# Hourglass attention and a phase MLP: four heads per load, two row blocks per store, and a new written order

## The chip, the cores and the metric

The kernel runs on one core of a Trainium2 chip. The core has five engines with queues of their own: TensorE (PE, matrix products, with its weight loads as PEld), VectorE (DVE), ScalarE (ACT), GpSimd (POOL) and SyncE (SP, which here only issues DMAs). The metric is the device time of one execution in microseconds (us).

## What is computed

```python
def sm_attn(qq, kk, vv):                      # softmax attention, scale 1/8
    ...
q_d = q.reshape(B, H, Sd, factor, D).mean(axis=3)      # factor 4; k_d, v_d alike
out_d = sm_attn(q_d, k_d, v_d)
out_up = np.repeat(out_d, factor, axis=2)
mask = np.abs(pos[:, None] - pos[None, :]) < factor    # local attention: 3 keys to either side
...
x = (out_up + out_local)                               # to (B, S, H * D)
theta = x @ w_theta
zr, zi = x * np.cos(theta), x * np.sin(theta)
u = x + np.einsum('ts,bsd->btd', w_tok_r, zr) + np.einsum('ts,bsd->btd', w_tok_i, zi)
return u + np.maximum(u @ w_ch, 0.0)
```

q, k and v are 8 batches x 8 heads x 576 positions x 64, in float32; the token weights are 576 x 576, the other weights 512 x 512; the result is 8 x 576 x 512 float32. The kernel computes in bfloat16 between loads and stores.

## The kernel before, in words

The program is written out in full, without loops at run time. Each kind of work is a generator that yields after each step, and a string, ORDER (L719), names the steps one letter at a time: the n-th occurrence of a letter runs the n-th step of its sequence (L749 to L756). Each step emits its instructions, and `pin` (L734) holds every engine to that order. So one string sets the order of PE, DVE, ACT, POOL and SP at once, and an instruction that waits holds up all that is behind it on its engine. A second string, BANKS (L63), names the PSUM bank (or the first of two) of each accumulator. The text below writes a step as its letter with the batch.

The steps, batch by batch:

- L (`load`, L182) issues the loads on SP: for k and q one DMA for two heads, 128 partitions x 576 float32, 288 KB, into a slot of the pool `stg` (16 slots, L60); for v five windows of 2 x 64 positions, each as two DMAs of 128 KB in rows of 64 values (`values`, L194). C (`cast`, L212) turns each loaded slot into bfloat16: in batch 0 on ACT (k), DVE (q) and POOL (v), afterwards all on POOL (L220, L224).
- A (`turns`, L290) transposes k and q on PE (L305), and ACT evacuates them (L306). a (`sums`) sums four neighbours for the pooled attention, on DVE (L334, L338) or POOL (L343, L344).
- S and P (L425, L401) are the local and the pooled scores with their exponentials on ACT; M (L433) multiplies the local ones by the band mask on DVE. U is the pooled v, V, y, N, x, n are the outputs, their quotients and a transposition; T (L537, L542) transposes and adds both to x.
- H (`phases`, L565 to L582) is x times w_theta, and cosine and sine of it on ACT. Its first step of a batch handles the last 64 positions (the tail) into the tile `cst`, which has one buffer. h (`tail_z`, L585) multiplies that by x into a tile `zT`, also with one buffer, and SP transposes it by a DMA (L591). Z (L617) makes the other z; in batches 6 and 7 the transposes for it are DMAs, J (L605).
- X (`mix`, L627) is the token mix, eight accumulations of nine matmuls of 256 or 320 columns for a batch (L638), each added to x on DVE (L642). r (`residual`, L645) turns the result back by four DMA transposes on SP (L652; in batch 7 on PE) and copies its tail on POOL (L656).
- R (`channels`, L669) multiplies by w_ch; O (`relu`, L689) takes max(.,0) and adds the residual on DVE (L692) into a slot `osb` of 128 x 512 float32, of which there are five; o (`store`, L708) stores each slot, 256 KB, on SP (L710). t, Q, q, s are the same for the tails of two batches at a time.
- l, c, w load, cast and transpose the weights in the same `stg` slots: w_theta first, then the token weights, and w_ch later.

ACT computes exponentials (S, P) and sines (H) from different function tables; a change from one to the other shows as an ACT_TABLE_LOAD.

A slot of a pool is taken by a new tile once the last reader of the old one is done; the first writer of the new one waits for that. `warm_up`, `more_values` and `storing` (L165, L204, L702) have no effect with the settings in this kernel, apart from one memset on DVE.

## Time and profile before

| | us |
|---|---|
| median of 3 runs | 240.19 (237.18 to 241.02) |
| the profiled execution: its time | 240.87 |
| the profiled execution: span from first to last instruction | 239.2 |
| PE busy | 215.0 |
| DVE busy | 191.6 |
| ACT busy | 152.0 |
| POOL busy | 104.6 |

The page of the profile gives each engine's busy time, the chain of work that ended last (followed back from the last instruction, at each step to what released it), and groups of instructions by line with their number, busy time and mean length. A busy PE is not a PE at its peak, since matmuls are pipelined and a waiting one can count as busy. The granted TensorE clock was 1.0 in the whole execution. In the chain and in the timelines a line begins with its start and its length in us; "SPq" is an issue on SP's queue, "issue" is time in which an engine waited for nothing that the profile shows.

### The profile page before, as it was taken

The page shows a single profiled execution, that of the slowest core. Times are in us where ns is not written, and L with a number is a line of the kernel's source. Part 1 is how long each engine was busy: PE and PEld are TensorE (multiplying, and loading weights), DVE is VectorE, ACT ScalarE, POOL GpSimd, SP SyncE. Part 2 cuts the span into 40 slices and gives each one's busy share as a digit, 9 for nine tenths or more (in the row PEclk, how much of TensorE's full clock was granted, in tenths as well). Part 3 has the DMA queues.
Part 4 walks back from the last instruction along what each step waited for, and adds up shares of the span by engine and source line. Part 5 has one row for each costly group of instructions (what it writes and reads, how often), then busy time and mean ns, then how long its engine had stood idle before and what let it go on. Part 6 is the DMA issues. An engine that isn't in the chain of part 4 may idle for free.

```text
span 239.2 us, 8218 instructions
## 1 busy us (share of the span) xinstructions
PE 215.0 (90%) x3370; PEld 154.3 (64%) x3370; DVE 191.6 (80%) x389; ACT 152.0 (64%) x212; POOL 104.6 (44%) x172
## 2 busy tenths in 40 slices
PE   0465998999899989989999999999999989999993
PEld 0443867777578765866577766866677557847751
DVE  5496889989778989866899898998999788665664
ACT  3678678969897886446884976377956953043030
POOL 6323636896857755377377324392163000000000
PEclk9999999999999999999999999999999999999999
DMA  6999999998999999999999939998876656473757
GB/s 201 266 182 321 357 311 159 260 279 157 292 216 217 228 282 185 183 235 299 202 192 277 302 63 210 233 230 223 134 179 109 86 118 180 83 222 67 206 177 256
DMA packets 84229, 50.11 MB, mean 210 GB/s; under 512 B 69216, under 2 KB 69216, under 8 KB 84192
## 3 DMA queue, kind: packets, MB, share of 16 engines
q1 hardware_dynamic: 84192, 49.60, 92.4%
q8 instruction: 26, 0.43, 0.8%
q14 instruction: 11, 0.09, 0.2%
HBM read 34.11 MB, written 9.44 MB: 182 GB/s over the span
## 4 chain that ended last, share of the span: by engine, by line
PE 68%; ACT 9%; DVE 7%; SPq 6%; DMA 3%; issue 3%; POOL 2%; DVEq 0%; ACTq 0%; POOLq 0%
PE psum L638 26%; PE psum L674 11%; PE psum L576 10%; PE psum L305 4%; PE psum L537 3%; SPq L198 3%; DMA st_v<-in_v_dram 2%; PE psum L497 2%; PE psum L616 2%; PE psum L445 2%; DVE tmp L514 2%; PE psum L452 2%; SPq L185 2%; ACT pm L425 1%; PE psum L418 1%
## 5 line engine op out<-in xcount | busy, mean ns | idle before, releaser
L638 PE MATMUL psum<-WT,z 128*128 128x256 bf16 (+1 forms) x576 | 77.0, 286 | 0.1
L638 PEld LDWEIGHTS <-z 128*128 128x128 bf16 x576 | 54.1, 98 | 14.8 <-issue 0.6
L642 DVE TENSOR_TENSOR uT<-psum,xT 128x256 bf16<-128x256 f32 (+1 forms) x64 | 28.9, 454 | 12.6 <-PE psum L638 11.8
L581 ACT ACTIVATE cs<-psum,pihc 128x512 bf16<-128x512 f32 x32 | 22.1, 691 | 21.4 <-PE psum L576 17.2
L224 POOL CAST v_w<-st_v 128x512 bf16<-128x512 f32 x40 | 24.8, 638 | 20.7 <-DMA st_v<-in_v_dram 19.1
L576 PE MATMUL psum<-wth,xT 128*128 128x512 bf16 x128 | 33.1, 387 | 0.1
L674 PE MATMUL psum<-wch,uT 128*128 128x512 bf16 x128 | 31.4, 379 | 0.7 <-ACT cs L582 0.7
L343 POOL TENSOR_TENSOR two<-qT 128x576 f32<-128x576 bf16 x14 | 16.1, 1147 | 27.6 <-ACT qT L306 27.4
L514 DVE TENSOR_TENSOR tmp<-psum,rl 128x512 bf16<-128x512 f32 x40 | 27.3, 684 | 0.7
L220 POOL CAST q_tm<-st_q 128x576 bf16<-128x576 f32 x28 | 21.6, 771 | 12.2 <-DMA st_q<-in_q_dram 11.9
L542 DVE TENSOR_TENSOR xT<-psum,xdT 128x464 bf16<-128x464 f32 (+1 forms) x40 | 24.5, 628 | 2.9 <-PE psum L537 2.5
L425 ACT ACTIVATE pm<-psum 128x1024 bf16<-128x1024 f32 (+1 forms) x24 | 20.5, 881 | 7.6 <-PE psum L418 6.8
L692 DVE SCALAR_TENSOR_TENSOR osb<-psum,ur 128x512 f32<-128x512 f32 x32 | 21.6, 684 | 2.3 <-PE psum L674 1.5
L306 ACT COPY qT<-psum 128x1152 bf16<-128x1152 bf16 x16 | 18.0, 1128 | 7.9 <-PE psum L305 7.9
L656 POOL COPY ut<-uT 128x256 bf16<-128x256 bf16 x8 | 3.4, 428 | 44.9 <-DVE uT L642 44.9
L334 DVE TENSOR_REDUCE kd<-kT 128x290 bf16<-128x1160 bf16 x16 | 21.6, 1353 | 1.6 <-ACT kT L306 1.6
L220 POOL CAST k_tm<-st_k 128x576 bf16<-128x576 f32 x28 | 19.5, 695 | 6.0 <-DMA st_k<-in_k_dram 5.3
L306 ACT COPY kT<-psum 128x1152 bf16<-128x1152 bf16 x16 | 17.9, 1122 | 5.6 <-PE psum L305 3.8
L305 PE MATMUL psum<-ident,k_tm 128*128 128x128 bf16 x144 | 11.9, 234 | 9.4 <-ACT k_tm L220 9.2
L674 PEld LDWEIGHTS <-uT 128*128 128x128 bf16 x128 | 11.8, 98 | 12.3 <-issue 0.8
L617 DVE TENSOR_TENSOR z<-psum,cs 128x1024 bf16<-128x1024 bf16 x24 | 16.3, 685 | 4.0 <-ACT cs L582 2.0
L582 ACT ACTIVATE cs<-psum 128x512 bf16<-128x512 f32 x32 | 19.1, 597 | 0.0
(87 smaller groups left out, 358.7 us busy)
## 6 DMA issues: line engine op xcount, KB each, us to landing
...
st_k<-in_k_dram SPq DMA_DIRECT2D x32, 288.0 KB, 4.9
st_q<-in_q_dram SPq DMA_DIRECT2D x32, 288.0 KB, 5.1
...
stw_tok<-in_moe_w_tok_r_dram SPq DMA_DIRECT2D x4, 288.0 KB, 6.6
stw_tok<-in_moe_w_tok_i_dram SPq DMA_DIRECT2D x4, 288.0 KB, 6.0
...
```

Of the source, the lines that this page charges most:

```text
L220: eng[i](out=dst[:, hh // 2, :, hh % 2, :], in_=staged.pop((b, f"{nm}{hh}")).rearrange("p (r d) -> p r d", d=D))
L224: eng[2](out=v_w[:, c, :, 0:D], in_=staged.pop((b, f"v{c}"))[:, 0:DM].rearrange("p (h d) -> p h d", d=D))
L306: EVAC[n](out=To[:, 2 * i:2 * i + 2, 0:S].rearrange("p a (w r) -> p a w r", r=WR), in_=ps[:, 0:P * WR].rearrange("p (r a w) -> p a w r", a ...
L334: nc.vector.tensor_reduce(out=kd_groups(kd)[:, 2 * i * NCH:2 * i * NCH + 2 * NCH, 0:PG], axis=AX.X, op=ALU.add, in_=kT[:, hs, :].rearrange ...
L425: nc.scalar.activation(out=pm.rearrange("p e c j w -> p e (c j w)"), in_=ps[:, :, 0:4 * W * n], func=AF.Exp, scale=SCL)
L514: nc.vector.tensor_tensor(out=tmp.rearrange("p g (j d) -> p g j d", d=D), in0=pv[:, :, :, 0:D], in1=rl.unsqueeze(3).to_broadcast([P, 2, 4, ...
L542: nc.vector.tensor_tensor(out=xT[:, :, CH * c:CH * c + cnt].rearrange("p e (m j) -> p e m j", j=4), in0=ps[:, :, 0:cnt].rearrange("p e (m ...
L576: nc.tensor.matmul(out=th, lhsT=xT[:, dc, P * c:P * c + P], rhs=wth[:, dc, :], start=(dc == 0), stop=(dc == 3),)
L581: nc.scalar.activation(out=cs[:, 0, :], in_=th, func=AF.Sin, bias=pihc, scale=1.0)
L638: nc.tensor.matmul(out=ps[:, 0:cnt], lhsT=z[:, j, P * dc:P * dc + P], rhs=WT[:, j, cols], start=(j == 8), stop=(j == 0),)
L642: nc.vector.tensor_tensor(out=uT[:, dc, cols], in0=ps[:, 0:cnt], in1=xT[:, dc, cols], op=ALU.add)
L674: nc.tensor.matmul(out=psr, lhsT=uT[:, dc, P * c:P * c + P], rhs=wch[:, dc, :], start=(dc == 0), stop=(dc == 3),)
```

## The change

1. From batch 1 on, one DMA loads four heads of k or q (576 KB) in place of two. Batch 0 keeps its loads.
2. The staging pool has 8 slots of two planes in place of 16 slots of one. k and q share a slot by two head pairs, v by windows (4), (3, 2), (1, 0), weights by two.
3. From batch 1 on, one cast on POOL handles a pair: 4 casts for k and q in place of 8, and 3 for v in place of 5.
4. Two blocks of 128 result rows share a slot of `osb`, three slots of 128 x 2 x 512, and one DMA stores both (512 KB); batch 7 still stores each block by itself. A tail block takes a whole slot.
5. `tail_z` writes its product into `cst` in place, so that `zT` has no tile of its own.
6. ORDER and BANKS are new throughout. In ORDER the letters v and D go, L has 76 steps in place of 104, C 62 in place of 104, o 18 in place of 32.
7. The code without effect is removed, with the memset.

```diff
-    stg = ctx.enter_context(tc.tile_pool(name="stg", bufs=16))
+    stg = ctx.enter_context(tc.tile_pool(name="stg", bufs=8))
...
-    def stage(b, key):
-        t = staged[b, key] = stg.tile([P, S], FP32, tag="st", name=f"st{b}_{key}")
-        return t
+    def stage(b, nm, i):
+
+        if (b, nm, i // 2) not in staged:
+            staged[b, nm, i // 2] = stg.tile([P, 2, S], FP32, tag="st", name=f"st{b}_{nm}{i // 2}")
+        return staged[b, nm, i // 2][:, i % 2, :]
 
     def load(b):
         for hh in range(4):
             for nm, src in (("k", k), ("q", q)):
-                nc.sync.dma_start(out=stage(b, f"{nm}{hh}"),
-                                  in_=src[b, 2 * hh:2 * hh + 2].rearrange("h (p r) d -> (h p) (r d)", r=WR))
-                yield
+                t = stage(b, nm, hh)
+                if b == 0:
+                    nc.sync.dma_start(out=t, in_=src[b, 2 * hh:2 * hh + 2].rearrange("h (p r) d -> (h p) (r d)", r=WR))
+                elif hh % 2 == 0:
+                    nc.sync.dma_start(out=staged[b, nm, hh // 2],
+                                      in_=src[b, 2 * hh:2 * hh + 4].rearrange("(x h) (p r) d -> (h p) x (r d)",
+                                                                              x=2, r=WR))
+                if b == 0 or hh % 2 == 0:
+                    yield
...
+                elif hh % 2 == 0:
+                    eng[i](out=dst[:, hh // 2].rearrange("p r e d -> p e r d"),
+                           in_=staged[b, nm, hh // 2].rearrange("p e (r d) -> p e r d", d=D))
+                    yield
...
+                lo, n = cs[-1], len(cs)
+                eng[2](out=v_w[:, lo:lo + n, :, 0:D],
+                       in_=staged[b, "v", lo // 2][:, 0:n, 0:DM].rearrange("p e (h d) -> p e h d", d=D))
+                yield
...
     def tail_z(b):
-        zT = moep.tile([P, 4, 2, HALF], BF16, tag="zT", bufs=1, name=f"zT_{b}")
+        zT = csts.pop(b)
...
     def relu(b):
         for c in range(4):
-            osb = osbs[b, c] = moep.tile([P, DM], FP32, tag="osb", bufs=5, name=f"osb{c}_{b}")
+            if c % 2 == 0:
+                osbs[b, c // 2] = moep.tile([P, 2, DM], FP32, tag="osb", bufs=3, name=f"osb{c}_{b}")
...
     def store(b):
         for c in range(4):
-            storing(b).dma_start(out=out[b, P * c:P * c + P, :], in_=osbs.pop((b, c)))
-            yield
+            osb = osbs[b, c // 2]
+            if b == B - 1:
+                nc.sync.dma_start(out=out[b, P * c:P * c + P, :], in_=osb[:, c % 2, :])
+                yield
+            elif c % 2 == 1:
+                nc.sync.dma_start(out=out[b, P * c - P:P * c + P, :].rearrange("(e p) d -> p e d", e=2), in_=osb)
+                yield
...
     ORDER = (
-        "LLLLCCLCACLLLLLlLaCCCAACaCLALaaSlMPVySLCcMSVyCMCCPUVlycllllNlVxcNLcLxcVccycLlCnTLCCCTyTwTwHTwHcAwZwH"
...
-        "yrLXyXLTrXLSSSLCoVhyoTXXLLLLTrTRHMZMHLHZZRHoOOaRACaaRZLOCAOCAXCAaXXVCCVyCPrLyaLLaUVMrLoSyPXraXNCNxCr"
...
-        "XTrTTXHoJJMCJCHJMCXhQVyqPRSVyMrrorOUXVrVoyVyHHNxNxRZHZnsTrZZyRRTHXToTTXXJJJJXXOXrhoXXOtOHRHooOZZRRHo"
-        "HRrQrrZZXXOXoOrXOXXrqXXrRrrRRrrOootsQROOqRsROoRoOOosROOooooo"
+        "lLLCLLLLLCCACLLAClCCLaLLLaCCLAAScaCSSlalcMCVPPCMClylVMVylUyllcCcLcVylNLxcNxcVAlnTcCTwTyHwHcwTTlZwcwl"
+        "wHcHwACwLLLwZZcHALchawCwwZwwwLwLwwXaLCLLAXLXLaLaCSSMCCXMSPCCLMXCPVVUyVyyNxNxAVAnLTyLLLXLHTTAAHHaaaaS"
+        "hVyXZCZCCSCMXPPTrVCULCTHLyNNxCHAxZZnAlTXXAaXAMaaCLLXXVSylLLalSXcCMPPcVrLyXlLTSSCVMyLrXHcTVyVChrUHCyH"
...
+        "rOORrRXsOXOnLStSTrXSaVPCMTyMCXXVyPVTXrrTToXyHJJVUyMXNJxNxJHhHVyVVRORoyOnTRTrZrHrZHHZZRTyTXXTXJXOJJJX"
+        "XhXXHHRORHZZHZZRORoXXoOQqXrrOXXrrOorXXXQRrrrtRroqrsOtOQRRRRsRRqOoOsOOOoOoooo"
     )
```

Three places of the new order, with letters resolved to steps (letter, batch, step within the batch; loads and casts left out), beside the old one:

```
about batch 2's first scores
before: X0.6 X0.7 y1.4 S2.0 r0.0 P2.0 S2.1 M2.0 P2.1 Z1.0 V2.0 U2.0 T1.4 H1.3
after:  S2.0 h1.0 V1.4 y1.4 X0.6 Z1.0 Z1.1 S2.1 M2.0 X0.7 P2.0 P2.1 T1.3 r0.0 V2.0 U2.0 T1.4 H1.3
about batch 7's scores and batch 6's phases (S, P and H alone)
before: S7.0 S7.1 P7.0 H6.0 H6.1 P7.1 S7.2 H6.2 H6.3 H6.4
after:  S7.0 S7.1 S7.2 P7.0 P7.1 H6.0 H6.1 H6.2 H6.3 H6.4
the first loads (SP)
before: k0 q0 k1 q1 k2 q2 k3 q3 v4 v3 theta0 v2 v1 v0 theta1
after:  theta0 k0 q0 k1 q1 k2 q2 k3 q3 v4 theta1 v3 v2 v1 v0
```

More of the change, by code (lines that the diff above doesn't have):

```diff
@@ L63 @@
     BANKS = (
-        "0240202460245020462345012346705234501423501634501234560134062046204623024062450145602146050240627645"
-        "0426304323426324062046320462320134621024601245012034615036123204632302460234501203420532043603623046"
-        "2306423402460324602546504236243024350246501240634304350365320462106724067062346534052635206134201240"
-        "63204632014051024124670246102410234502362703202010140123452323010102301302401201"
+        "0240204620462304206452345263470123540612305103456731240563124026124601240264012301460124607416204106"
+        "7206423702630243204630462304623046120312467016207612302024604134024016204620145672356037452304304260"
+        "4526045206420620463245301340256702546540724650450264026540214260526401520642034672304273016403121460"
+        "24062320463201304123042304620123042501425142121212301241525205023230145012301456"
     )
@@ L159 @@
     PU = [PU[0], PU[1], PU[1], PU[1], PU[2]]
-    warm = const.tile([P, 256], BF16, name="warm")
-    nc.vector.memset(warm, 0.0)
-    def warm_up():
-        for i, n in enumerate(WARM):
-            ps = w1(f"wu{i}")
-            for _ in range(n):
-                nc.tensor.matmul(out=ps[:, 0:256], lhsT=ident, rhs=warm, start=True, stop=True)
-            yield
-    WARM = []
     staged, inputs = {}, {}
-    def stage(b, key):
-        t = staged[b, key] = stg.tile([P, S], FP32, tag="st", name=f"st{b}_{key}")
-        return t
+    def stage(b, nm, i):
+        if (b, nm, i // 2) not in staged:
+            staged[b, nm, i // 2] = stg.tile([P, 2, S], FP32, tag="st", name=f"st{b}_{nm}{i // 2}")
+        return staged[b, nm, i // 2][:, i % 2, :]
     def load(b):
@@ L184, in load @@
             for nm, src in (("k", k), ("q", q)):
-                nc.sync.dma_start(out=stage(b, f"{nm}{hh}"),
-                                  in_=src[b, 2 * hh:2 * hh + 2].rearrange("h (p r) d -> (h p) (r d)", r=WR))
-                yield
+                t = stage(b, nm, hh)
[7 more added lines that the diff above has]
+                    yield
         for c in BACK:
-            if HALVES[b] > 0:
-                stage(b, f"v{c}")
-                values(nc.sync, b, c, range(HALVES[b]))
-                yield
+            stage(b, "v", c)
+            values(nc.sync, b, c, range(2))
+            yield
     def values(queue, b, c, halves):
-        t = staged[b, f"v{c}"][:, 0:DM].rearrange("p (h d) -> p h d", d=D)
+        t = stage(b, "v", c)[:, 0:DM].rearrange("p (h d) -> p h d", d=D)
         for g in halves:
@@ L198, in values @@
             queue.dma_start(out=t[W * g:W * g + W], in_=v[b, :, lo:lo + W, :].rearrange("h p d -> p h d"))
-    HALVES = [2, 2, 2, 2, 2, 2, 2, 2]
-    def more_values(b):
-        for c in BACK:
-            if HALVES[b] < 2:
-                if HALVES[b] == 0:
-                    stage(b, f"v{c}")
-                values(nc.scalar, b, c, range(HALVES[b], 2))
-                yield
     def cast(b):
@@ L219, in cast @@
             for i, (nm, dst) in enumerate((("k", k_tm), ("q", q_tm))):
-                eng[i](out=dst[:, hh // 2, :, hh % 2, :],
-                       in_=staged.pop((b, f"{nm}{hh}")).rearrange("p (r d) -> p r d", d=D))
+                if b == 0:
+                    eng[i](out=dst[:, hh // 2, :, hh % 2, :],
+                           in_=stage(b, nm, hh).rearrange("p (r d) -> p r d", d=D))
+                    yield
[3 more added lines that the diff above has]
+                    yield
+        for cs in UNITS:
+            if b == 0:
+                for c in cs:
+                    eng[2](out=v_w[:, c, :, 0:D], in_=stage(b, "v", c)[:, 0:DM].rearrange("p (h d) -> p h d", d=D))
+                    yield
+            else:
+                lo, n = cs[-1], len(cs)
+                eng[2](out=v_w[:, lo:lo + n, :, 0:D],
+                       in_=staged[b, "v", lo // 2][:, 0:n, 0:DM].rearrange("p e (h d) -> p e h d", d=D))
                 yield
-        for c in BACK:
-            eng[2](out=v_w[:, c, :, 0:D], in_=staged.pop((b, f"v{c}"))[:, 0:DM].rearrange("p (h d) -> p h d", d=D))
-            yield
     CASTS = {0: (act, dve, gp), None: (gp, gp, gp)}
@@ L239, in wide_weight @@
         for i in range(4):
-            nc.sync.dma_start(out=stage("w", f"{nm}{i}")[:, 0:DM], in_=w[P * i:P * i + P, :])
+            nc.sync.dma_start(out=stage("w", nm, i)[:, 0:DM], in_=w[P * i:P * i + P, :])
             yield
@@ L244, in weight_loads @@
         yield from wide_weight(moe_w_theta, "th")
-        for ri, ct in TOK:
-            t = stage("w", f"tok{ri}{ct}")
+        for i, (ri, ct) in enumerate(TOK):
+            t = stage("w", "tok", i)
             if ct < 4:
@@ L256, in weight_casts @@
         for i in range(4):
-            act(out=wth[:, i, :], in_=staged.pop(("w", f"th{i}"))[:, 0:DM])
+            act(out=wth[:, i, :], in_=stage("w", "th", i)[:, 0:DM])
             yield
         for i, (ri, ct) in enumerate(TOK):
-            (gp, act)[i % 2](out=w_tm[ri][:, ct, :], in_=staged.pop(("w", f"tok{ri}{ct}")))
+            (gp, act)[i % 2](out=w_tm[ri][:, ct, :], in_=stage("w", "tok", i))
             yield
         for i in range(4):
-            gp(out=wch[:, i, :], in_=staged.pop(("w", f"ch{i}"))[:, 0:DM])
+            gp(out=wch[:, i, :], in_=stage("w", "ch", i)[:, 0:DM])
             yield
@@ L585, in tail_z @@
     def tail_z(b):
-        zT = moep.tile([P, 4, 2, HALF], BF16, tag="zT", bufs=1, name=f"zT_{b}")
+        zT = csts.pop(b)
         nc.vector.tensor_tensor(
-            out=zT, in0=xTs[b][:, :, 512:576].unsqueeze(2).to_broadcast([P, 4, 2, HALF]), in1=csts.pop(b), op=ALU.mult,
+            out=zT, in0=xTs[b][:, :, 512:576].unsqueeze(2).to_broadcast([P, 4, 2, HALF]), in1=zT, op=ALU.mult,
         )
@@ L690, in relu @@
         for c in range(4):
-            osb = osbs[b, c] = moep.tile([P, DM], FP32, tag="osb", bufs=5, name=f"osb{c}_{b}")
-            nc.vector.scalar_tensor_tensor(out=osb, in0=rels.pop((b, c)), scalar=0.0, in1=urs[b][:, c, :],
+            if c % 2 == 0:
+                osbs[b, c // 2] = moep.tile([P, 2, DM], FP32, tag="osb", bufs=3, name=f"osb{c}_{b}")
+            nc.vector.scalar_tensor_tensor(out=osbs[b, c // 2][:, c % 2, :], in0=rels.pop((b, c)), scalar=0.0, in1=urs[b][:, c, :],
                                            op0=ALU.max, op1=ALU.add)
@@ L696, in tail_relu @@
     def tail_relu(i):
-        osb = osbs["t", i] = moep.tile([P, DM], FP32, tag="osb", bufs=5, name=f"osbt_{i}")
+        osb = osbs["t", i] = moep.tile([P, 2, DM], FP32, tag="osb", bufs=3, name=f"osbt_{i}")[:, 0, :]
         nc.vector.scalar_tensor_tensor(out=osb, in0=rels.pop(("t", i)), scalar=0.0,
@@ L700, in tail_relu @@
         yield
-    def storing(b):
-        return nc.scalar if b in BY_ACT else nc.sync
-    BY_ACT = ()
     def store(b):
         for c in range(4):
-            storing(b).dma_start(out=out[b, P * c:P * c + P, :], in_=osbs.pop((b, c)))
-            yield
+            osb = osbs[b, c // 2]
+            if b == B - 1:
+                nc.sync.dma_start(out=out[b, P * c:P * c + P, :], in_=osb[:, c % 2, :])
+                yield
+            elif c % 2 == 1:
+                nc.sync.dma_start(out=out[b, P * c - P:P * c + P, :].rearrange("(e p) d -> p e d", e=2), in_=osb)
+                yield
     def tail_store(i):
@@ L715, in tail_store @@
         for e in range(2):
-            storing(2 * i + 1).dma_start(out=out[2 * i + e, 512:576, :], in_=osb[HALF * e:HALF * e + HALF])
+            nc.sync.dma_start(out=out[2 * i + e, 512:576, :], in_=osb[HALF * e:HALF * e + HALF])
         yield
     ORDER = (
-        "LLLLCCLCACLLLLLlLaCCCAACaCLALaaSlMPVySLCcMSVyCMCCPUVlycllllNlVxcNLcLxcVccycLlCnTLCCCTyTwTwHTwHcAwZwH"
-        "CHllhclalLLLLLcccLCZwHwZLwwACwwCwwwLwwZLwALLwaAaLLLXCLLXSMaSXMSVyCLCPCCLCCXVCyPLVMUyCXNxCNLLALCAxVCn"
-        "TXLTyHLTAChaLHAaLaHCTCLVaXLCXySLrCPCSMCPZCVUTHyNZHCAxCCZNALZMXLLXCCAaCXlAaalXxLXLSLLVCCyacrMLCCCCSXc"
-        "PlrLVSMlyLnXVSCyPTXrTCrHTTLLVLyVUHyhAcNCcNxCTaHMAMxRZHLCORRHOCZCZAOZRLLLLLLOnLXACTCXXHVCyCCCoLrCCrVV"
-        "yrLXyXLTrXLSSSLCoVhyoTXXLLLLTrTRHMZMHLHZZRHoOOaRACaaRZLOCAOCAXCAaXXVCCVyCPrLyaLLaUVMrLoSyPXraXNCNxCr"
-        "xXSVoLMCCyPXnToSPMCVyUXTNHTHLLLhrACxTLROLoLLrLoZNHxTaCZHALCCROHCAZZRROCaVCyVVtMXyXXAanCrXLLLyrXVSySO"
-        "aXTLXMCTVCMCCCSPyUTrLXVyVLLPQqyoHoNThRrHCLoTCNCrxHOCxCZRMAZaHtoAOnHRZOAZaaLRALaXOXTXVSyVyXCTLCVSrryP"
-        "XTrTTXHoJJMCJCHJMCXhQVyqPRSVyMrrorOUXVrVoyVyHHNxNxRZHZnsTrZZyRRTHXToTTXXJJJJXXOXrhoXXOtOHRHooOZZRRHo"
-        "HRrQrrZZXXOXoOrXOXXrqXXrRrrRRrrOootsQROOqRsROoRoOOosROOooooo"
+        "lLLCLLLLLCCACLLAClCCLaLLLaCCLAAScaCSSlalcMCVPPCMClylVMVylUyllcCcLcVylNLxcNxcVAlnTcCTwTyHwHcwTTlZwcwl"
+        "wHcHwACwLLLwZZcHALchawCwwZwwwLwLwwXaLCLLAXLXLaLaCSSMCCXMSPCCLMXCPVVUyVyyNxNxAVAnLTyLLLXLHTTAAHHaaaaS"
+        "hVyXZCZCCSCMXPPTrVCULCTHLyNNxCHAxZZnAlTXXAaXAMaaCLLXXVSylLLalSXcCMPPcVrLyXlLTSSCVMyLrXHcTVyVChrUHCyH"
+        "TTcNZCLZMLMxHZHNxROLZRrRLnrCORXXXTCXLLAOOoCXVyVXyALXLACArTHCrroLVVyLyXahSarSMSRaHLCLaLRLTTTOCRHOZHLA"
+        "OZZHLAaRCZMAXXOAXVPyLCaPMXoXSCVaaSUryXCVyrrCSrPXLNNxxXCLMCVPVrnRyUTTORTRyLHACLLOhTOTLHNAZHHHxLaZNZCA"
+        "axZROXCaALorXMXVSSytMXLVrVSCryCLayonXMCCTATXVPVLyyXrLCaPoVyUHTXLTNLxhAMaMHNZAQxCHLTHVyVqyRZZarHrZRAr"
+        "rOORrRXsOXOnLStSTrXSaVPCMTyMCXXVyPVTXrrTToXyHJJVUyMXNJxNxJHhHVyVVRORoyOnTRTrZrHrZHHZZRTyTXXTXJXOJJJX"
+        "XhXXHHRORHZZHZZRORoXXoOQqXrrOXXrrOorXXXQRrrrtRroqrsOtOQRRRRsRRqOoOsOOOoOoooo"
     )
@@ L749 @@
     sequences = dict(
-        L=each(load), v=each(more_values), C=each(cast), l=weight_loads(), c=weight_casts(), w=weight_turns(), D=warm_up(),
+        L=each(load), C=each(cast), l=weight_loads(), c=weight_casts(), w=weight_turns(),
         A=each(turns), B=each(settle, TURNED_QK), J=each(turn_x, TURNED_X), a=each(sums), U=each(pooled_v),
```

## The prediction

> **What bounds the kernel now.** I read, in this order, the busy shares and the chain of work that ended last, the table of 10 us stretches, the chain in order of time, and the timelines of ACT, DVE and SP.

> ```profile
> span 239.2 us, 8218 instructions
> ...
> PE 215.0 (90%) x3370; PEld 154.3 (64%) x3370; DVE 191.6 (80%) x389; ACT 152.0 (64%) x212; POOL 104.6 (44%) x172
> ...
> PE 68%; ACT 9%; DVE 7%; SPq 6%; DMA 3%; issue 3%; POOL 2%; DVEq 0%; ACTq 0%; POOLq 0%
> ```

> PE is nearly full, and DVE is a close second. POOL, which does the casts that change, is under half busy and has 2% of the chain. To see what is left on PE I charged each step of the order with the shortest time that its kind takes in the trace from the end of the PE step before it to its own end (0.98 and 1.22 us for the two sizes of a mix step, 0.86 for a channel step). That gives 193 us of PE work. PE's first step ends at 8.8 us, its last at 235.4, and 3.8 us follow, so some 34 us are waits between steps: 24.7 from 10 to 90 us (2.8 of it from 60 to 70), 8.6 from 70 to 180, 2.6 from 180 to 200, and next to nothing from there on.

> ```profile
> 60.00:70.00 10.00, 8.71 (x172) 6.08 (x170) 7.09 (x16) 9.00 (x14) 7.90 (x13) 1.00 1.13 269
> ...
> 110.00:120.00 10.00, 10.00 (x85) 6.08 (x84) 7.92 (x13) 7.01 (x11) 5.03 (x8) 1.00 1.05 228
> ...
> 190.00:200.00 10.00, 9.21 (x129) 5.55 (x128) 8.63 (x19) 6.03 (x11) 0.40 (x1) 1.00 0.55 131
> ```

> The columns are PE, PEld, DVE, ACT and POOL busy, then the granted clock (full throughout), the DMA share and GB/s. At 60 to 70 us ACT is the fullest (9.00) while PE waits; at 110 PE is at its limit.

> ```profile
> 15.69 4.85 DMA st_v<-in_v_dram
> 20.66 0.63 POOL v_w L224
> 21.33 0.64 PE psum L355 x4
> ...
> 42.07 3.27 DMA st_k<-in_k_dram
> ...
> 61.14 0.56 ACT L425
> 61.70 0.74 issue
> 62.44 0.60 ACT pm L425
> ...
> 183.88 1.28 ACT L570
> ...
> 187.00 1.28 ACT L401
> ```

> Loads stand on the chain up to 21 us (batch 0, whose loads keep their size) and once more for 3.27 us at 42. From there on it is PE, ACT and DVE. At 61 and from 183 to 196 us ACT holds it, with table loads.

> **The change, part by part.** The sum is made against the profiled execution's own time, 240.87 us (span 239.2 and 1.7 around it); that is 0.7 above the median shown, 240.19.

> *SP queue.* All DMAs are issued by SP, 190 us of issuing in 239. 28 of 64 k/q issues go (mean 0.51 us), and 14 of 32 stores (0.53): 28 x 0.51 + 14 x 0.53 = 21.7 us less, if one of double size costs what one costs now; if it costs twice, nothing is saved.

> ```profile
> 98.86 0.38 SPq L185 DMA_DIRECT2D st_q<-in_q_dram  x1
> ...
> 100.97 3.90 SPq L652 DMA_TRANSPOSE ur<-uT  x3
> ```

> SP mostly runs ahead of the engines: these transposes of batch 1 were issued 13 to 16 us before relu asked for them at 116.8. What SP saves is therefore hidden behind PE: 0. Without that cover the 3.27 us at 42 would be the gain, and that is a rival.

> *Transfers.* The bytes are the same.

> ```profile
> st_k<-in_k_dram SPq DMA_DIRECT2D x32, 288.0 KB, 4.9
> ...
> ur<-uT SPq DMA_TRANSPOSE x28, 4.9
> ```

> One load takes 4.9 us to land, but issues follow each other by 0.47 us, so several are in flight at once and their fixed part overlaps: 0. [...]

> *POOL.* A cast of 576 columns takes 0.67 us and one of 512 takes 0.62 when undisturbed, so 64 columns cost 0.05 and about 0.18 is fixed. 56 k/q casts become 28 of 1152 and 35 v casts become 21 (14 of 1024): (28 + 14) x 0.18 = 7.6 us less of POOL's 104.6. It idles over half the time: 0 on the path. A pair waits for both its halves, but the casts stand tens of steps ahead of their transposes.

> ```profile
> 78.39 1.14 DVE L433 TENSOR_TENSOR pm<-pm,band 128x1024 bf16<-128x1024 bf16 x1
> ```

> Against it: the mask product took 1.14 us here beside a v cast, and 0.68 alone; of the 16 full ones four lie above 0.8. A doubled cast can hold it for longer: from 0 to the same excess again, about 1.2 us of DVE in all; I take +0.3, since most of the 24 are undisturbed. [...]

> *Buffers.* 8 pairs hold what 16 single slots held. Followed along the order, 12 of 16 were in use at most; now all 8 are, at batch 2's v loads, which are issued 9 steps after the batch 1 cast that frees their slot. SP would stand there until POOL gets to it, about 43 us, which is when batch 2's loads are issued now (42.07): 0. The in-place z tail makes the next batch's sin wait for the transposing DMA (2.9 us to land); the nearest pair, batches 6 and 7, is still 6.2 us of PE work apart: 0. Three pairs of output rows replace five rows. The last batch stores as before, but batch 6's rows 256 to 511 go out 512 KB at once, right ahead of it: 256 KB more in the last slice at its 256 GB/s would be 1.0 us, hidden if the queue drains faster; +0.3.

> *Order, 0 to 45 us.* A theta load now goes ahead of the first k load. 256 KB at the second slice's 266 GB/s is 1.0 us, its issue 0.45; k and q land about 0.7 late. ACT then evacuates the second transpose (1.12) before it casts the last two k loads, so batch 0's scores come about 1.5 us late at 16.9. They meet the v loads, which have two theta loads ahead instead of one: +0.6 at 21.33. Towards the first mix step the new order has 1.4 us less DVE work (one pooled sum of 1.35 moves behind it), and DVE is 90% busy there. Between -1.3 and +1.9, nearest to the balance: 0.

> *Order, 60 to 70 us.* Before, batch 2's first scores (S) came after batch 0's last mix step, so that ACT's table load and exponentials ran while the next PE step waited for their banks. Now S comes before the last two mix steps (2.2 us of PE work). PE lost 2.8 us here; between 0 and -2.8, and DVE has 1.9 us more work before this place, so half: -1.5.

> *Order, 180 to 200 us.* Sin and exp follow each other in 18 runs now, in 16 then: all exponentials of batch 7 stand ahead of batch 6's sins.

> ```profile
> 187.00 1.28 ACT L401 ACT_TABLE_LOAD   x1
> ...
> 192.98 1.28 ACT L581 ACT_TABLE_LOAD   x1 [1.64 <-PE psum L576]
> ```

> These two go, 2.6 us of ACT where ACT holds the chain. PE lost 2.6 us in these 20 us, so 0 to -2.6; next in line is DVE (8.63 of 10), so -1.5.

> *The rest of the order.* PE work ahead of each batch's first mix step differs by under 2 us between the orders, and reuse of a PSUM bank within 1 us of PE work falls from 50 cases to 31 of 500: 0.

> Sum: 0.3 + 0.3 - 1.5 - 1.5 = -2.4, so 238.5 by the profiled time, and 237.8 by the median, which I give.

> **The rivals.**
> *Transposes too late (slower).* In the order, the last residual transpose stands 7.7, 10.7 and 9.3 us of PE work ahead of relu in batches 0 to 2; now 6.9, 5.3 and 5.8. In batch 2 all four stand within 1.6 us of PE work, the first 7.4 ahead of relu: three more issues of 1.26 and the last one's landing are 3 x 1.26 + 4.9 = 8.7 us. If SP reaches them only at their place in the order, DVE waits 1.3 us there, with all that is behind it; in batch 1 it is 2 x 1.26 + 4.9 less 6.0, 1.4 us. At 1.4 in three batches: 237.8 + 4.2 = 242.0, and 3 more for each us that a landing takes above the median, or 1.9 more with the head. It decides when SP is less than 8.7 us ahead. For it: the distances. Against it: SP has less to issue and has run ahead.
> *Loads were the bound (faster).* If landing earlier pays, the 3.27 us at 42 go too: 234.5. For it: SP's 80% and POOL's 19.1 us of waits for v loads. Against it: after 48 us no load is on the chain. [...]
> *Given back (no change).* The late head stays (+1.9), or the new gaps at ACT only move: 239.7 to 240.2. For it: DVE has 1.9 us more work before 62 us.

> **How the numbers follow.** Forecast 0.45 (own range 235.5 to 240.0), transposes late 0.20, loads the bound 0.20, given back 0.15. A difference of 2% is about what a measurement here can tell from none: below 235.4 or above 245.0. Faster 0.22 (most of the loads rival and the forecast's lower end), slower 0.16 (most of the transposes rival, with landings a us over the median or the late head), same 0.62. The range 234.0 to 244.0 takes in both rivals and the forecast, and leaves out about 0.2.

> **What would show it.** 16 table loads, none between 185 and 195 us; PE's loss at 60 to 70 and 180 to 200 us each lower by about 1.5; the first mix step near 44 us; about 170 us of issuing on SP and 97 busy on POOL, with no waits of PE for POOL in their place. DVE relu waiting for a transposing DMA in batches 0 to 2 would show the first rival, an earlier arrival at 48 us the second. The forecast is wrong if the first mix step is over 1.5 us late, or if PE's loss from 70 to 180 us, 8.6 us now, grows.

## The result, and the profile after

The changed kernel takes 241.35 us (median of 22 runs) against 239.41 us of the kernel before (22 runs; each has one far outlier, 259.0 and 729.0 us): the ratio is 1.0084, 95% interval 1.0057 to 1.0111. The forecast was 237.8 us. The time lies inside the range, but the sign is the other one: a little slower, not a little faster. The profiled execution took 242.48 us, with a span of 240.8. Each ratio in this text is taken over fast runs alone, those within 1.5% of the fastest run of the same kernel, while each median is over all runs, so the one is not the quotient of the others; e9 below has only two such runs, and its ratio is that of the medians.

The first lines of the page of the changed kernel, and its chain of work that ended last by engines:

```profile
span 240.8 us, 8075 instructions
...
PE 214.2 (89%) x3370; PEld 152.7 (63%) x3370; DVE 193.6 (80%) x388; ACT 148.5 (62%) x210; POOL 97.8 (41%) x130
...
PE 58%; DMA 13%; DVE 11%; SPq 7%; issue 4%; ACT 4%; POOL 2%; DVEq 0%; POOLq 0%; ACTq 0%
```

PE does the same work in a longer span, ACT and POOL do less, and the DMA share of the chain went from 3% to 13%, PE's from 68% to 58%. Of the 31.5 us of DMA on the chain 20.5 are three loads between 56.9 and 87.1 us. That is no measure of a loss: PE's loss from 60 to 70 us fell, as the next lines say, and behind the last of the three it waits 1.2 us (below, at 88 us). The table of 10 us stretches tells where (columns as in the prediction):

```profile
60.00:70.00 10.00, 9.89 (x152) 7.45 (x151) 7.59 (x17) 9.52 (x14) 4.99 (x6) 1.00 1.24 240
110.00:120.00 10.00, 10.00 (x99) 7.13 (x97) 9.37 (x15) 8.54 (x13) 6.80 (x7) 1.00 1.35 215
...
130.00:140.00 10.00, 8.56 (x119) 5.38 (x120) 6.94 (x15) 3.75 (x6) 3.45 (x4) 0.83 0.99 220
150.00:160.00 10.00, 8.19 (x233) 6.46 (x234) 8.40 (x18) 5.33 (x6) 5.14 (x5) 1.00 1.31 229
...
190.00:200.00 10.00, 9.84 (x136) 5.90 (x134) 8.88 (x20) 4.71 (x11) 0.40 (x1) 1.00 0.68 133
```

The same table of the kernel before has for the two middle ones:

```profile
130.00:140.00 10.00, 9.84 (x223) 7.33 (x220) 8.60 (x19) 8.10 (x13) 3.69 (x5) 1.00 0.91 191
150.00:160.00 10.00, 9.67 (x211) 7.66 (x210) 9.19 (x19) 5.21 (x6) 6.38 (x10) 1.00 1.32 258
```

At 60 and 190 us PE is fuller than before, as forecast. At 130 and 150 us every engine is emptier (ACT at 150 alone is not), and at 130 the granted clock is 0.83. Charged as in the prediction (each step's time less the shortest of its kind), PE loses 20.7 us from its start to 80 us where it lost 23.3, then 12.9 from 80 to 180 where it lost 7.6, then 1.8 from 180 to 200 where it lost 2.6. So 3.4 us are won and 5.3 are lost again in the middle.

The biggest loss there is one step. The timeline of PE in the changed kernel (start, duration, then what; in brackets the idle time before and what ended it):

```profile
128.25 0.44 PE L439 MATMUL psum<-vd,pd 128*72 128x65 bf16 x8
128.52 0.34 PE L446 MATMUL psum<-ve,pd 128*72 128x130 bf16 x3
131.44 0.25 PE L446 MATMUL psum<-ve,pd 128*72 128x130 bf16 x1 [2.58 <-issue]
131.53 1.73 PE L632 MATMUL psum<-WT,z 128*128 128x320 bf16 x7
```

Three of four equal matmuls run, and the fourth comes after 2.58 us of idle time. It waits for no semaphore that the profile shows: the bracket says "issue". The fourth reads the same tiles as the third, so a late operand is unlikely. Afterwards the granted clock is 0.5 from 131.9 to 135.3 us, which is the 0.83 of the table. A candidate for the cause is on the DMA side, a queue of its own, of the kind "instruction" (the share is of 16 engines' span, here of 2 us from 128 to 130):

```profile
q8 instruction: 1, 0.02, 3.7%
```

One packet of 16,384 bytes, from 128.64 to 129.83 us. There are 26 of them in either kernel, and PE runs 2 x 3370 = 6740 matmuls and weight loads: 259 for each. I take them for PE's instructions, and estimate from these counts that one packet brings about 256, or 128 matmuls with their weight loads: the four stalls of the changed kernel at 54.72, 131.44, 156.35 and 163.37 us come after 734, 2014, 2398 and 2526 matmuls, whole multiples of 128 apart, and with 128 instructions more (e4 below) there are 27 packets. I call these 128 matmuls a block.

Two other losses looked like waits for engines. PE stands for 1.72 us before a mix step at 156.35 us, and the timelines of PE and DVE name a late copy on DVE:

```profile
156.35 1.16 PE L632 MATMUL psum<-WT,z 128*128 128x256 bf16 x9 [1.72 <-DVE xdT L476]
```

```profile
155.83 0.45 DVE L476 COPY xdT<-psum 128x576 bf16<-128x576 bf16 x1
```

The copy ends at 156.28, the matmul starts at 156.35: it fits. It is wrong, as the second experiment showed. And at 88 us PE waits for a weight cast that POOL could not start before a paired q cast, which waited 2.43 us for its 576 KB load:

```profile
87.18 1.63 POOL L207 CAST q_tm<-st_q 128x1152 bf16<-128x1152 f32 x1 [2.43 <-DMA st_q<-in_q_dram]
88.76 0.61 POOL L257 CAST wch<-stw_ch 128x512 bf16<-128x512 f32 x1
```

### The profile page after: what moved, and what is told of

It is laid out like the page before. It is cut to its first block, busy times and chain, and to the rows that moved or that the text cites. A ratio compares the mean times of both kernels' runs of the same rounds, so it can differ in the third digit from the quotient of the medians.

```text
span 240.8 us, 8075 instructions
## 1 busy us (share of the span) xinstructions
PE 214.2 (89%) x3370; PEld 152.7 (63%) x3370; DVE 193.6 (80%) x388; ACT 148.5 (62%) x210; POOL 97.8 (41%) x130
## 4 chain that ended last, share of the span: by engine, by line
PE 58%; DMA 13%; DVE 11%; SPq 7%; issue 4%; ACT 4%; POOL 2%; DVEq 0%; POOLq 0%; ACTq 0%
PE psum L632 18%; PE psum L668 11%; PE psum L570 8%; DMA st_q<-in_q_dram 8%; DMA st_v<-in_v_dram 5%; PE psum L299 4%; SPq L192 3%; PE psum L531 2%; PE psum L491 2%; PE psum L446 2%; DVE uT L636 2%; DVE tmp L508 2%; PE psum L678 1%; DVE z L611 1%; PE psum L610 1%
## 5 line engine op out<-in xcount | busy, mean ns | idle before, releaser
L632 PE MATMUL psum<-WT,z 128*128 128x256 bf16 (+1 forms) x576 | 78.6, 288 | 1.8 <-DVE xdT L476 1.7
L668 PE MATMUL psum<-wch,uT 128*128 128x512 bf16 x128 | 31.5, 380 | 1.2 <-POOL wch L257 1.2
L570 PE MATMUL psum<-wth,xT 128*128 128x512 bf16 x128 | 31.4, 379 | 0.0
L300 ACT COPY kT<-psum 128x1152 bf16<-128x1152 bf16 x16 | 18.1, 1133 | 18.5 <-DVE uT L636 9.8
L508 DVE TENSOR_TENSOR tmp<-psum,rl 128x512 bf16<-128x512 f32 x40 | 26.8, 682 | 0.5
L217 POOL CAST v_w<-st_v 128x1024 bf16<-128x1024 f32 (+1 forms) x21 | 19.3, 920 | 18.2 <-DMA st_v<-in_v_dram 15.8
L207 POOL CAST q_tm<-st_q 128x1152 bf16<-128x1152 f32 x14 | 16.6, 1183 | 19.8 <-DMA st_q<-in_q_dram 19.7
L337 POOL TENSOR_TENSOR two<-qT 128x576 f32<-128x576 bf16 x14 | 17.7, 1265 | 13.6 <-ACT qT L300 13.5
L419 ACT ACTIVATE pm<-psum 128x1024 bf16<-128x1024 f32 (+1 forms) x24 | 20.0, 881 | 5.0 <-PE psum L412 4.9
L207 POOL CAST k_tm<-st_k 128x1152 bf16<-128x1152 f32 x14 | 16.1, 1149 | 17.1 <-DMA st_k<-in_k_dram 16.9
L395 ACT ACTIVATE pd<-psum 128x864 bf16<-128x864 f32 x16 | 13.7, 897 | 9.6 <-PE psum L374 9.6
L576 ACT ACTIVATE cs<-psum 128x512 bf16<-128x512 f32 x32 | 19.3, 602 | 0.0
## 6 DMA issues: line engine op xcount, KB each, us to landing
st_k<-in_k_dram SPq DMA_DIRECT2D x4, 288.0 KB, 5.0
st_q<-in_q_dram SPq DMA_DIRECT2D x4, 288.0 KB, 5.0
stw_tok<-in_moe_w_tok_r_dram SPq DMA_DIRECT2D x4, 288.0 KB, 6.1
stw_tok<-in_moe_w_tok_i_dram SPq DMA_DIRECT2D x4, 288.0 KB, 6.6
```

The lines of the kernel that those rows point to most:

```text
L207: eng[i](out=dst[:, hh // 2].rearrange("p r e d -> p e r d"), in_=staged[b, nm, hh // 2].rearrange("p e (r d) -> p e r d", d=D))
L300: EVAC[n](out=To[:, 2 * i:2 * i + 2, 0:S].rearrange("p a (w r) -> p a w r", r=WR), in_=ps[:, 0:P * WR].rearrange("p (r a w) -> p a w r", a ...
L508: nc.vector.tensor_tensor(out=tmp.rearrange("p g (j d) -> p g j d", d=D), in0=pv[:, :, :, 0:D], in1=rl.unsqueeze(3).to_broadcast([P, 2, 4, ...
L570: nc.tensor.matmul(out=th, lhsT=xT[:, dc, P * c:P * c + P], rhs=wth[:, dc, :], start=(dc == 0), stop=(dc == 3),)
L632: nc.tensor.matmul(out=ps[:, 0:cnt], lhsT=z[:, j, P * dc:P * dc + P], rhs=WT[:, j, cols], start=(j == 8), stop=(j == 0),)
L668: nc.tensor.matmul(out=psr, lhsT=uT[:, dc, P * c:P * c + P], rhs=wch[:, dc, :], start=(dc == 0), stop=(dc == 3),)
```

## The experiments

Three theories stood against each other. *A*: PE's instruction fetches come late behind the larger transfers, and a long one costs clock besides. *B*: the new order itself loses the time, by PE's waits for DVE and POOL. *C*: pairs land later, so casts and data come late (in the second round: the paired casts cost it). *D*, added later: it is only where the stalls happen to fall. The kernels e1 to e14 were each timed in five rounds beside the kernel before on the same chip, whose medians were 239.8 to 240.5 us. The profiled executions of e2, e4 and e6 were 1.5, 3.7 and 1.6 us above the medians of their kernels, those of e7, e10 and e12 1.3 to 1.4 us below, so a sum over one trace is a sample and not a mean.

In the table, "stalls" is the sum over PE's idle times of more than 0.35 us, from 25 to 172 us, that end a block and end 1.2 to 1.75 us after a fetch has landed. In two traces of the old order some matmul records are missing, and the count runs a little short. "Delay" is the mean time from PE's entering a block to the start of the fetch of the next one, in the same stretch (new order only, where blocks are matched with certainty). "Low clock" is the number of runs with a mean granted clock below 0.9955, whatever pause came before.

| kernel | k/q loads | median us | ratio to before | stalls us | delay us | low clock |
|---|---|---|---|---|---|---|
| before | 288 KB | 239.41 to 240.46 | 1 | 1.85 | | 16 of 98 |
| changed | 576 KB | 241.35 | 1.0084 (1.0057 to 1.0111) | 5.59 | 2.78 | 17 of 22 |
| e1 changed again | 576 KB | 241.86 | 1.0094 (1.0055 to 1.0132) | 5.35 | 2.69 | 7 of 12 |
| e2 order alone | 288 KB | 238.67 | 0.9940 (0.9901 to 0.9979) | 2.65 | 2.10 | 6 of 12 |
| e3 pairs, old order | 576 KB | 255.32 | 1.0643 (1.0597 to 1.0690) | 4.14 | | 6 of 6 |
| e4 changed, 64 ahead | 576 KB | 239.61 | 0.9975 (0.9935 to 1.0015) | 3.59 | 2.24 | 3 of 12 |
| e5 loads single | 288 KB | 239.81 | 1.0008 (0.9959 to 1.0056) | 2.27 | 1.71 | 9 of 12 |
| e6 casts single | 576 KB | 242.43 | 1.0135 (1.0061 to 1.0210) | 5.76 | 2.60 | 3 of 6 |
| e7 order alone, 64 ahead | 288 KB | 237.70 | 0.9958 (0.9913 to 1.0002) | 1.49 | 2.00 | 2 of 12 |
| e8 before, 64 ahead | 288 KB | 241.05 | 1.0073 (1.0028 to 1.0119) | 1.10 | | 0 of 12 |
| e9 changed, 96 ahead | 576 KB | 243.94 | 1.017 of medians, no interval | 5.02 | 2.45 | 3 of 6 |
| e10 loads, stores single | 288 KB | 239.25 | 0.9945 (0.9901 to 0.9988) | 2.48 | 1.75 | 6 of 12 |
| e11 as e10, 64 ahead | 288 KB | 239.80 | 0.9989 (0.9948 to 1.0031) | 0.39 | 1.77 | 3 of 12 |
| e12 stores single | 576 KB | 242.72 | 1.0051 (0.9990 to 1.0113) | 4.42 | 2.60 | 12 of 12 |
| e13 old order, paired loads | 576 KB | 244.14 | 1.0147 (1.0101 to 1.0193) | 5.17 | | 3 of 6 |
| e14 old order, paired stores | 288 KB | 252.19 | 1.0476 (1.0419 to 1.0533) | 0.71 | | 6 of 6 |

**e1, the changed kernel again.** No edit.

> The changed kernel again. In its first trace PE lost 2.8 us inside one step (the second pooled output step of batch 4, at 129 us), with no semaphore as releaser, while a 16 KB fetch of instructions landed; the granted clock was 0.5 for the 3.4 us that followed. Theory A (fetches of PE's instructions come late behind the larger transfers, and a long one costs clock besides): the stall stands at the same step again, the mean clock is near 0.993 in most runs, ratio to before 1.006 to 1.011. Theory B (the new order itself loses the time, by waits of PE for DVE and POOL): the ratio is the same, but the stall at that step is gone or under 1 us in this trace, and the waits for DVE in batch 4 (1.9 us) and for POOL in batch 0 (1.4 us) stand. Theory C (pairs land later, and data come late): the ratio is the same, and the casts wait for loads.

The stall stands at the same matmul, between the third and the fourth of the same step:

```profile
129.77 0.34 PE L446 MATMUL psum<-ve,pd 128*72 128x130 bf16 x3
131.99 0.25 PE L446 MATMUL psum<-ve,pd 128*72 128x130 bf16 x1 [1.88 <-issue]
```

Here the clock drop came after the other long stall (1.80 us at 153.6, clock 0.5 from 155.8 to 159.2), and none after this one. The wait for POOL at 88 us is gone, and the time is still that of the changed kernel, which speaks against theories B and C as to that wait. (e2, which is faster, has it again, 1.36 us at 89.8.)

**e2, the order alone.** Each paired load, cast and store becomes two single ones at the same place:

```diff
-                    nc.sync.dma_start(out=staged[b, nm, hh // 2], in_=src[b, 2 * hh:2 * hh + 4]...)
+                    for x in range(2):
+                        nc.sync.dma_start(out=staged[b, nm, hh // 2][:, x, :], in_=src[b, 2 * (hh + x):2 * (hh + x) + 2]...)
```

and likewise for casts and stores.

> The new order, banks and paired buffers, but with each paired load, cast and store issued as two single ones at the same place in the order. Theory A: the fetches stand behind 288 KB loads as before, the long stall goes, and the gains of the order stay: ratio 0.985 to 0.995 (236 to 238.2 us). Theory B: the loss stays with the order: 1.005 to 1.011 (240.6 to 242). Theory C: as A, 0.985 to 0.995, but because the casts no longer wait.

0.9940, with an interval wholly below 1: the new order is faster than the old one, and the pairs cost 1.0084/0.9940, that is 1.4%, or 3.5 us (with both intervals, 1.0% to 1.9%, 2.3 to 4.6 us). Theory B is out. The step at 130 us now stalls 0.40 us. The stall before the mix step stays, and shows that its label misleads (PE, then DVE):

```profile
153.90 2.10 PE L634 MATMUL psum<-WT,z 128*128 128x256 bf16 x9 [2.25 <-DVE xdT L478]
```

```profile
152.53 0.45 DVE L478 COPY xdT<-psum 128x576 bf16<-128x576 bf16 x1
```

DVE's copy ends at 152.98, and PE stands until 153.90. What it shares with the stall at 130 us is the count: counted from the start, 2014 and 2398 matmuls, both 94 modulo 128 (the expectation of e5 counts one less), and the fetch landed 1.41 us before PE went on (1.61 at 131.44 in the changed kernel). In all the kernels of the table, every idle time over 0.35 us at that count (95 in some traces of the old order) ends 1.2 to 1.75 us after a landing. And in the new order no block at all, stalled or not, is entered sooner than 1.18 us after its own packet has landed.

**e3, the pairs in the old order.** The order and bank list of before; a paired load stands at the first of its two places, a paired cast and store at the second.

> The order and the banks of before, with the paired loads (at the place of the first of the two), the paired casts (at the place of the second), the paired stores and buffers of the change. Theory A: mid-step stalls without a releaser grow beyond the 1.3 us of before: 1.003 to 1.012 (240 to 242.3 us). Theory B: nothing is lost by the pairs: 0.997 to 1.003. Theory C: slower as in A, 1.005 to 1.015, with waits of PE for POOL's casts behind the later loads.

15 us slower, far outside what any theory said. 8.7 of them are one wait of PE that begins at 195 us, so this run told little of the rest; e13 and e14 take it apart.

**e4, 64 matmuls ahead.** The count of instructions is shifted by half a block, and nothing else:

```diff
+    for _ in range(64):
+        nc.tensor.matmul(out=psum[:, 7, 0:1], lhsT=ident, rhs=ident[:, 0:1], start=True, stop=True)
     pin()
     for s in ORDER:
```

They end at 3.3 us, and PE then still waits 4.8 us for ACT's first cast.

> The changed kernel with 64 matmuls of one column ahead of its first transpose, while PE has nothing to do: 128 instructions more, half of the 256 that one fetch brings. Nothing else moves but the places in the order where a fetch ends. Theory A: the stall of 2.8 us leaves its step; the stalls stand some 64 matmuls from where they stood, and with the long one gone the clock stays at 1.0: ratio 0.99 to 1.003 (237 to 240 us), or another long one at another place. Theories B and C: the same ratio as the changed kernel, 1.006 to 1.011, and the stalls stand where they stood.

0.9975 instead of 1.0084 and 1.0094: more instructions, and 2 us less. The stalls at both old places are gone (0.40 us is left before the mix step, at another count); others, up to 1.72 us, stand 64 matmuls earlier or a whole number of blocks from there, all at counts of 94 modulo 128. The step that stalled runs through, and a score step 64 matmuls ahead of the old place stalls:

```profile
130.03 0.36 PE L412 MATMUL psum<-qT,kT 64*64 64x64 bf16 x20 [1.08 <-issue]
...
132.29 0.40 PE L446 MATMUL psum<-ve,pd 128*72 128x130 bf16 x4
```

Theories B and C cannot explain it. D can, as far as it goes: place matters.

**e5 and e6, loads single and casts single.** The edit of e2 for the loads alone, and for the casts alone.

> The changed kernel with each paired k or q load issued as two of 288 KB, one right behind the other; stores and casts stay paired. In the runs so far PE stood 1.35 to 1.7 us beyond the landing of a 16 KB instruction fetch at every stall that ends at the same count of matmuls (93 modulo 128), and the fetch began up to 4.9 us after the block before it was entered. Theory A (the fetches queue behind the large loads): the delays of the fetches return to those of the kernel before (mean 2.0 to 2.1 us), the stall at 129 us falls below 1 us, and the time falls by most of what pairing costs in the new order (1.5%): ratio to before 0.994 to 0.999. Theory C (the paired casts cost it, through POOL's holding of DVE or a later start): no change from the changed kernel, 1.006 to 1.011. Theory D (nothing but where the stalls happen to fall): anything from 0.99 to 1.01, with delays no shorter.

> The changed kernel with each paired cast made as two of 576 (or 512) columns, one right behind the other; loads and stores stay paired. Theory A: no change from the changed kernel, 1.005 to 1.011, and the stall at 129 us stays over 1.5 us. Theory C: most of the 1.5% comes back, 0.994 to 0.999. Theory D: anything from 0.99 to 1.01.

With single loads the ratio falls to 1.0008 (its interval ends just below that of the changed kernel), the delay of the fetches from 2.7 to 1.71 us, and the stall at 130 us from 2.58 and 1.88 to 1.16:

```profile
132.06 0.25 PE L446 MATMUL psum<-ve,pd 128*72 128x130 bf16 x1 [1.16 <-issue]
```

With single casts nothing comes back (1.0135, in a wide interval that holds the changed kernel's 1.0084). Theory C in its second form is out. Theory A missed in its numbers: the stall stayed over 1 us, and the ratios are above the 0.994 to 0.999 named for e5 and the 1.005 to 1.011 named for e6, though both intervals reach into these ranges.

**e7 and e8, 64 ahead in the order alone and in the kernel before.** The edit of e4.

> The new order with single loads, casts and stores, and 64 matmuls of one column ahead of PE's first transpose. The stall left in the new order with single transfers was one of 2.25 us at 152 us, in the block of 128 matmuls that takes only some 3 us of PE work, with the clock at 0.5 after it. Theory A: the block ends elsewhere, this stall goes and the clock drop with it; another of about 1 us may come: 0.983 to 0.992 (236 to 238 us). Theory B (that stall is a wait for DVE's copy, as the trace names it): the stall stays, 0.992 to 0.997.

> The kernel before with 64 matmuls of one column ahead of PE's first transpose; nothing else. Theory A: the stalls of 1.0 and 0.8 us at 107 and 84 us leave their steps, others come where a block falls on the score and output steps: 0.993 to 1.007. If it is over 1.007, the position of the blocks alone is worth as much as the change; if the time is the same within 0.3%, the kernel before is not sensitive to it, and the sensitivity came with the change.

In e7, PE passes the place of the mix step without a pause, behind the same DVE copy:

```profile
150.37 0.45 PE L493 MATMUL psum<-v_w,pm 64*64 64x65 bf16 x32
150.65 0.46 PE L414 MATMUL psum<-qT,kT 64*64 64x64 bf16 x32
151.04 0.43 PE L475 MATMUL psum<-ident,xd 72*128 72x72 bf16 x8
151.31 1.15 PE L634 MATMUL psum<-WT,z 128*128 128x256 bf16 x9
```

So that stall was a fetch, and not DVE. Those lines also show why blocks run short there: 32 score matmuls of 64 columns take 0.46 us, so 128 matmuls of such steps pass in some 3 us (3.1 in the changed kernel, from 151.53 us to the start of the pause at 154.63). The ratio (0.9958) is no better than that of e2 within the intervals, though the median is 1 us less. It misses theory A's 0.983 to 0.992 and lies in the range named for theory B; what decides against B is the trace, where the stall is gone. The kernel before becomes 0.7% slower by the same edit, just over the 1.007 at which the expectation calls the place alone worth as much as the change. Its trace does not show the loss (1.10 us of stalls against 1.85), so the cause of its 1.7 us is not shown.

**e9, 96 ahead.** The edit of e4 with 96. From the stall-free times of e7 one can add up how far the blocks fall short of a given time, for any shift. That sum was least near 56 to 64 and greatest near 96 to 104.

> The changed kernel with 96 matmuls of one column ahead of PE's first transpose, where 64 gave a ratio of 0.9975. From the times of PE's matmuls in the run without long stalls (new order, single transfers, 64 matmuls ahead), the blocks of 128 matmuls between 25 and 172 us that would take less than 6.0 us fall short of it by 7.5 us in all with none ahead, by 4.7 with 64 and by 10.2 with 96. Theory A: 2.7 us more than the changed kernel and 5.5 more than with 64: about 244 us, ratio 1.012 to 1.025, with stalls near 78, 82, 107 and 125 us. Theory D or any theory in which the dummy matmuls themselves help (a warmer clock, say): as with 64, 0.995 to 1.002.

The median is 243.94 us, as worked out (about 244). But the six runs spread from 240.09 to 247.50 us and give no interval, so the size is not settled. The longest stall is where one was expected, behind 80 score matmuls:

```profile
107.50 0.89 PE L412 MATMUL psum<-qT,kT 64*64 64x64 bf16 x80
111.01 1.51 PE L668 MATMUL psum<-wch,uT 128*128 128x512 bf16 x4 [2.62 <-DVE cst L581]
```

Again the label is an engine's, and the landing (109.6) is 1.4 us before. Of the four places named, only this one came true; the other stalls are at 51, 160 and 166 us.

**e10, e11 and e12, stores.** Single loads and stores with paired casts; the same with 64 ahead; single stores alone.

> The changed kernel with both paired loads and paired stores issued as two single ones; only the casts (and the buffers) are paired. Theory A: the same as the new order with all single, 0.991 to 0.997, since casts put no bytes in the queues. If it stays at 1.000 or above, as with the loads alone single (1.0008), the paired casts cost something in the company of single loads, and the stores nothing.

> As the run with single loads and stores and paired casts, with 64 matmuls of one column ahead of PE's first transpose. Theory A: as the all-single kernel with 64 ahead (0.9958) or a little under it, 0.985 to 0.996: the version that should beat both kernels. If the paired casts cost, over 0.997.

> The changed kernel with the paired stores alone issued as two of 256 KB; loads and casts stay paired. Theory A: a small part of the gain, since loads are most of the bytes in flight: 1.002 to 1.009, with delays of the fetches (mean 2.6 to 2.8 us) a little shorter. If all of the loss is from the stores, 0.995 to 1.001.

e10 has the ratio of e2: with single transfers the paired casts show no cost beyond the intervals of 0.4%, and they take 7 us of work off POOL (97.3 us busy, against 104.5 in e2). What stores alone cost is not settled by e12: its ratio of 1.0051 is not separated from the changed kernel, and its median is even higher than the changed kernel's, 1.012 of the kernel before. e11 missed: it has the least stalls of all, 0.39 us, and is not the fastest. Its 0.9989 lies where its expectation says that the paired casts cost something; e10 and e6 speak against that, and the intervals do not decide it. Stalls of one profiled execution rank the kernels only roughly (rank correlation with the ratio 0.61 over the table without e3 and e14).

**e13 and e14, one part each in the old order.** Paired loads alone; paired stores with three pairs of output rows alone.

> The order of before with paired loads and paired staging buffers alone (the load at the place of the first of the two); casts and stores are single, at their old places. Theory A: the mean delay of the fetches rises from 1.5 to 2.1 us, as in all kernels with single loads so far, to 2.2 to 2.8, as in all with paired ones; the kernel before has few blocks that are short of time, so it costs 0.5 to 2.5 us: ratio 1.002 to 1.012. Theory C (the loads in pairs land too late for the old order): over 1.015, with PE waiting for POOL's casts.

> The order of before with the paired stores, three pairs of output rows and the in-place z tail alone; loads and casts are single. If the paired output rows made the 15 us of the run with all pairs under the old order, this one shows DVE's relu waiting some 8 us for a store at 190 to 200 us and a ratio of 1.03 to 1.06. If they did not: 0.998 to 1.01.

The two together, 1.0147 and 1.0476, make up the 1.0643 of e3. e13 is above the 1.012 that theory A allowed and just short of theory C's 1.015, but C's sign is missing: after 25 us PE waits for a cast of POOL for 0.24 us at most. In e13 one of three long stalls is this, in the middle of six matmuls of one step:

```profile
47.27 0.40 PE L342 MATMUL psum<-v_w,pu 128*32 128x512 bf16 x3 [0.24 <-POOL v_w L211]
49.78 0.39 PE L342 MATMUL psum<-v_w,pu 128*32 128x512 bf16 x1 [2.12 <-issue]
```

with 1.55 at 86.6 and 1.50 at 110.3 us beside it: 5.17 us against 1.85 in the kernel before, 3.3 more, where the median rose by 3.7. But the mean delay of the fetches, which I had expected at 2.2 to 2.8, is about 1.8, as without pairs: in the old order the mean does not carry it. By the count, which runs a little short here, more of them are late: 6 of 18 start over 3 us behind the entry, against 2 of 18 in the kernel before. In e14, DVE and SP show the wait:

```profile
197.98 0.69 DVE L693 SCALAR_TENSOR_TENSOR osb<-psum,ur 128x512 f32<-128x512 f32 x1 [8.92 <-DMA out_dram<-osb]
```

```profile
189.64 5.10 SPq L652 DMA_TRANSPOSE ur<-uT  x3
194.79 0.58 SPq L716 DMA_DIRECT2D out_dram<-osb  x1
```

With three pairs, relu needs the pair whose store stands on SP behind three transposes. In the old order that costs 9 us; in the trace of the changed kernel DVE's relu never waits for a store.

## Why the prediction was wrong

The step that failed is *Transfers*, "One load takes 4.9 us to land, but issues follow each other by 0.47 us, so several are in flight at once and their fixed part overlaps: 0". As to a gain that held: larger transfers brought none. But PE's instructions come by DMA too (26 packets of 16 KB in the trace), and the step did not ask what larger transfers do to them. Measured: the pairs cost 3.5 us in the new order (changed kernel against e2), of which single loads give back about 1.8 (e5); single stores on top of these give about 1.5 more (e10), which the intervals do not separate from nothing, and single casts give nothing (e6). With paired loads in the new order PE's fetches start 2.2 to 2.8 us behind the entry of the block in the mean, with single ones 1.7 to 2.1. The traces show 5.6 and 5.4 us of fetch stalls with pairs and 2.7 without; of the 5.3 us lost from 80 to 180 us they are 3.4 (5.2 now, 1.8 before). A lower clock goes with longer runs: in the changed kernel the five runs at 0.997 or more have a median of 239.97 us, the ten at 0.992 and 0.993 one of 241.52. Whether the clock or the pause ahead of it takes that time, no run separates, and not every drop follows a fetch: in the traces of e5 and e12 the clock fell after a pause of 1.3 us that ended at 48.4 and 48.5 us, at another count.

- *SP queue.* A paired issue costs little more than a single one did (0.58 against 0.51 us for loads, 0.73 against 0.53 for stores), so most of the 21.7 us should have gone. The sum stayed: 190.4 us in 248 issues became 191.8 in 206. The v issues went from 0.76 to 0.92 us and the residual transposes from 1.35 to 1.59. The expected 170 us were wrong; the price of 0 on the path was right.
- *Transfers.* The landing times grew, and not only of what was paired. The changed kernel:

```profile
st_v<-in_v_dram SPq DMA_DIRECT2D x80, 128.0 KB, 6.3
st_k<-in_k_dram SPq DMA_DIRECT2D x14, 576.0 KB, 7.0
...
out_dram<-osb SPq DMA_DIRECT2D x14, 512.0 KB, 3.7
```

  And the kernel before:

```profile
st_v<-in_v_dram SPq DMA_DIRECT2D x80, 128.0 KB, 4.9
```

  So a v load of unchanged size took 4.9 us before and 6.3 now. Only part of that goes with the pairs: in the new order it is 5.2 to 5.6 us with single loads (e2, e5, e10) and 5.9 to 6.3 with paired ones (changed kernel, e1, e6, e12; 5.6 in e4), and in the old order paired loads left it at 4.5 (e13).
- *POOL.* 97.8 us busy, as said (97.0), and no cost on the path that e6 shows. The one longer wait of PE for it after 25 us, 1.2 us for a weight cast at 89.4 us, is as long with single casts (1.36 us in e2).
- *Mask contention, +0.3.* mask products above 0.8 us went from 4 of 24 to 9, and all 24 together from 16.0 to 18.8 us, more than the 1.2 us that the prediction allowed for at most. It goes with the casts: 18.1 to 19.8 us where they are paired (changed kernel, e1, e5, e10), 16.3 and 16.8 where they are single (e6, e2). DVE is busy 2.0 us longer; what of it reaches the end is within the intervals of e6 and e10. *Tail, +0.3*: 3.8 us in both, so 0.
- *Order.* -1.5 and -1.5 were said. At 60 to 70 us the loss fell by 1.8, at 180 to 200 by 0.8, and the head, priced at 0, gained: the first mix step starts at 38.5 us instead of 41.6 (the 44 of the prediction was too late for both). ACT loads 16 tables instead of 18, as said, but one at 188.4 us, where none was to be. Together e2 measures -1.4 us (between -0.5 and -2.4) for the order and its buffers: right in sign, and about half of the 3.0.
- *The place named as fatal,* PE's loss from 70 to 180 us, did grow, from 8.6 us to 13.7. *Transposes too late* was the rival with the right sign and the wrong mechanism: DVE's relu waits 1.41 us for a transpose in batch 0 (91.3 us), and PE loses 0.1 at most there. *Loads were the bound* is out: larger loads made it slower.

What stays open: how larger transfers hold a fetch back, and which ones do. The fetch for the stall at 131 us started at 128.64, just as the 512 KB store landed (128.63); but with that store split (e12) the stall is still 2.09. Transposes and loads were in flight with it, and no run takes these apart. Also open are e8's loss and why e11 is not the fastest.

Two versions beat the kernel before with their whole intervals: the new order with single transfers (e2, 0.9940) and the same with paired casts (e10, 0.9945). Nothing here separates the two; e2 with 64 matmuls ahead (e7) has the lowest median, 237.70 us, but an interval up to 1.0002.
